# Threshold attention and a quick-GELU feed-forward in float32: scores transposed, values stationary for two heads, row maximum over partitions, tanh for sigmoid, 512-token blocks

## Chip, cores, metric

One core of one Trainium2 chip. The metric is the device time of one execution in microseconds (us), as the median of a kernel's fast runs.

## The reference

```python
q, k, v: (8, 8, 576, 64) float32;  tau = 0.02
scores = q @ k.T / 8
thresh = max(scores, -1) - tau
scores = where(scores >= thresh, scores, -1e9)
attn   = softmax(scores, -1)                    # the sum has 1e-9 added
x      = (attn @ v) as (4608 tokens, 512)
h      = x @ w_in                               # 512 x 2048
out    = (h * sigmoid(1.702 * h)) @ w_out       # 2048 x 512
```

The weights arrive as float64 words and are rounded to float32 on the chip. All matmuls run in float32.

## The kernel before

Queries lie on the partitions of the scores. A step handles 128 queries of two heads: scores, row maximum over the free dimension, exp, threshold with the row sum as accumulator, ten transposes of the weights on TensorE, then the values with the transposed weights stationary. Feed-forward units of batch b are woven between the steps of batch b+1.

```python
def row_max(sc):                                   # scores: queries x keys, in PSUM
    for h in range(2):
        nc.vector.tensor_reduce(out=nmax[:, h:h+1], in_=sc[h][:, :, 0:SH],
                                axis=AXL.XY, op=ALU.max, negate=True)
    ...
def exps(sc, bias):     # ScalarE: exp(scl * score + bias), from PSUM
def threshold(sc, thr, w):
    nc.vector.scalar_tensor_tensor(out=w[h], in0=sc[h][:, :, 0:SH], scalar=thr[:, h:h+1],
        in1=w[h], op0=ALU.is_ge, op1=ALU.mult, accum_out=den[:, h:h+1])
def transpose_w(w):     # 2 heads x (4 + 1) TensorE transposes of 128 x 128, then copies
def values(n, t, wT, rcp):
    for h in range(2):
        for c in range(NT):
            nc.tensor.matmul(pv[:, h, :], lhsT=wT[:, h, c, :], rhs=vr[:, h, ts(c, D)], ...)
    nc.vector.tensor_tensor(out=x, in0=pv, in1=rcp.to_broadcast([P, 2, D]), op=ALU.mult)
def gelu():                                        # after mm1 of one 128 x 384 hidden tile
    nc.scalar.activation(out=sig, in_=hps, func=AF.Sigmoid, scale=GELU_SCALE)
    nc.vector.tensor_tensor(out=gT[j], in0=hps, in1=sig, op=ALU.mult)
```

## Time and profile before

| | kernel before |
|---|---|
| median | 1957.6 us |
| TensorE busy | 96% |
| start, until the first feed-forward matmul | 258 us |
| middle, attention and feed-forward together | 1522 us |
| end, feed-forward alone | 175 us |

In the middle TensorE is busy 99.6% of the time, so TensorE's work sets the time there. The lines are in the prediction. PE is TensorE, DVE VectorE, ACT ScalarE, POOL GpSimd; PEclk is the share of the clock that TensorE was granted, in tenths; "idle before" on a line is how long the engine stood still just ahead of such instructions, and the arrow names what ended the wait.

### The profile page before, as it was taken

How to read it: one execution, taken by the hardware profiler on the slowest of the kernel's cores; microseconds unless marked ns; L12 is line 12 of the kernel's file. 1: busy time of each engine (PE TensorE's matmuls, PEld its weight loads, DVE VectorE, ACT ScalarE, POOL GpSimd, SP SyncE). 2: the span in 40 equal slices, each digit the busy share in tenths (PEclk: the TensorE clock that was granted, in tenths of full speed). 3: DMA queues.
4: the chain of work that ended last, by engine and by line, in shares of the span. 5: the costliest groups of instructions: out<-in, count | busy, mean ns of one | idle time of the engine just before them, and what ended most of it. 6: DMA issues, size and time to landing. Idle time of an engine off the chain costs nothing.

```text
span 1955.3 us, 23581 instructions
## 1 busy us (share of the span) xinstructions
PE 1870.5 (96%) x9248; PEld 1252.2 (64%) x9248; DVE 985.8 (50%) x2216; ACT 712.1 (36%) x1066; POOL 149.3 (8%) x422
## 2 busy tenths in 40 slices
PE   6776799999999999999999999999999999999999
PEld 4565677666666667666656667766656667766554
DVE  6888765555344355555435345555434445553110
ACT  2222255335325245334425336434424325432010
POOL 2333200000000000000000000000000000000000
PEclk8556599999999999999999999999999999999999
DMA  4323210101010000001010010000001010000000
GB/s 123 100 76 94 61 31 15 29 19 30 12 30 13 18 24 19 24 24 28 16 29 19 12 30 19 24 24 24 19 11 26 22 30 19 1 11 6 11 6 17
DMA packets 100160, 56.06 MB, mean 29 GB/s; under 512 B 83152, under 2 KB 91344, under 8 KB 100048
## 3 DMA queue, kind: packets, MB, share of 16 engines
q1 hardware_dynamic: 100048, 54.55, 10.0%
q8 instruction: 73, 1.20, 0.3%
q14 instruction: 39, 0.32, 0.1%
HBM read 45.09 MB, written 9.44 MB: 28 GB/s over the span
## 4 chain that ended last, share of the span: by engine, by line
PE 88%; DVE 9%; ACT 1%; issue 1%; POOL 1%; DMA 0%; SPq 0%; DVEq 0%; POOLq 0%; ACTq 0%
PE hps L310 25%; PE ops L329 25%; PE pv L278 16%; PE sc L204 9%; PE w_ps L261 7%; DVE frac L147 3%; PE x_ps L296 2%; PE w_ps L270 2%; DVE w L244 1%; DVE ex L173 1%; DVE qT L188 1%; DVE nmax L216 1%; PE qk_ps L187 1%; DVE ex L161 1%; DVE frac L143 1%
## 5 line engine op out<-in xcount | busy, mean ns | idle before, releaser
L310 PE MATMUL hps<-xT,w_in 128*128 128x384 f32 x1536 | 524.1, 487 | 0.0
L329 PE MATMUL ops<-w_out,gT 128*128 128x512 f32 x1152 | 515.7, 593 | 0.0
L278 PEld LDWEIGHTS pv<-v_raw,wT 128*128 128x128 f32 x3200 | 410.4, 206 | 46.8 <-DVE wT L262 14.2
L278 PE MATMUL pv<-v_raw,wT 128*128 128x64 f32 x3200 | 411.5, 287 | 10.9 <-DVE wT L262 10.1
L310 PEld LDWEIGHTS hps<-xT,w_in 128*128 128x128 f32 x1536 | 279.4, 190 | 161.4 <-issue 0.5
L329 PEld LDWEIGHTS ops<-w_out,gT 128*128 128x128 f32 x1152 | 209.5, 190 | 217.9 <-issue 217.1
L216 DVE TENSOR_REDUCE nmax<-sc 128x1 f32<-128x576 f32 x320 | 227.5, 752 | 145.0 <-PE sc L204 143.9
L234 ACT ACTIVATE w<-sc,bias,scl 128x576 f32<-128x576 f32 x320 | 248.5, 827 | 30.1 <-POOL bias L222 19.6
L244 DVE SCALAR_TENSOR_TENSOR w<-sc,thr,w 128x576 f32<-128x576 f32 x320 | 247.5, 811 | 6.9 <-ACT w L234 6.7
L204 PE MATMUL sc<-kT,qT 64*128 64x288 f32 x1280 | 219.9, 459 | 4.1 <-DVE w L244 3.8
L271 DVE COPY wT<-w_ps 128x256 f32<-128x256 f32 x160 | 67.6, 423 | 298.3 <-PE w_ps L270 298.3
L298 ACT COPY xT<-x_ps 128x128 f32<-128x128 f32 x128 | 50.5, 395 | 440.0 <-PE x_ps L296 440.0
L318 DVE TENSOR_TENSOR gT<-hps,sig 128x384 f32<-128x384 f32 x192 | 106.9, 557 | 177.0 <-ACT sig L317 170.8
L317 ACT ACTIVATE sig<-hps 128x384 f32<-128x384 f32 x192 | 94.1, 490 | 252.4 <-PE hps L310 250.4
L261 PE MATMUL w_ps<-ident,w 128*128 128x128 f32 x1280 | 177.9, 285 | 0.0
L204 PEld LDWEIGHTS sc<-kT,qT 64*128 64x128 f32 x1280 | 124.8, 201 | 57.7 <-issue 35.0
L261 PEld LDWEIGHTS w_ps<-ident,w 128*128 128x128 f32 x1280 | 156.5, 149 | 0.8 <-issue 0.8
L222 POOL TENSOR_SCALAR bias<-nmax,scl 128x2 f32<-128x2 f32 x160 | 41.7, 261 | 1338.7 <-DVE nmax L216 1297.0
L262 ACT COPY wT<-w_ps 128x512 f32<-128x512 f32 x160 | 94.1, 588 | 88.3 <-PE w_ps L261 88.3
L283 DVE TENSOR_TENSOR x<-pv,rcp 128x128 f32<-128x128 f32 x160 | 45.5, 284 | 143.7 <-PE pv L278 143.7
L270 PEld LDWEIGHTS w_ps<-ident,w 128*128 128x128 f32 x320 | 44.5, 145 | 104.2 <-issue 48.7
L262 DVE COPY wT<-w_ps 128x512 f32<-128x512 f32 x160 | 108.9, 681 | 1.1 <-PE w_ps L261 1.1
(44 smaller groups left out, 834.4 us busy)
## 6 DMA issues: line engine op xcount, KB each, us to landing
out_dram<-osb SPq DMA_DIRECT2D x36, 256.0 KB, 2.0
q_raw<-in_q_dram SPq DMA_DIRECT2D x64, 128.0 KB, 2.8
k_raw<-in_k_dram SPq DMA_DIRECT2D x64, 128.0 KB, 2.7
v_raw<-in_v_dram SPq DMA_DIRECT2D x32, 256.0 KB, 2.9
w<-in_moe_w_in_dram SPq DMA_DIRECT2D x16, 512.0 KB, 3.8
w<-in_moe_w_out_dram SPq DMA_DIRECT2D x16, 512.0 KB, 3.4
q_raw<-in_q_dram SPq DMA_DIRECT2D x32, 32.0 KB, 2.5
k_raw<-in_k_dram SPq DMA_DIRECT2D x32, 32.0 KB, 2.5
```

Of the source, the lines that this page charges most:

```text
L204: nc.tensor.matmul(sc[h][:, c, 0:SH], lhsT=qT[rows, ds(T0[t], P)], rhs=kT[rows, ts(c, SH)], start=True, stop=True,)
L216: nc.vector.tensor_reduce(out=nmax[:, h : h + 1], in_=sc[h][:, :, 0:SH], axis=AXL.XY, op=ALU.max, negate=True,)
L234: nc.scalar.activation(out=e, in_=sc[h][:, :, 0:SH], func=AF.Exp, bias=bias[:, h : h + 1], scale=scl,)
L244: nc.vector.scalar_tensor_tensor(out=w[h], in0=sc[h][:, :, 0:SH], scalar=thr[:, h : h + 1], in1=w[h], op0=ALU.is_ge, op1=ALU.mult, accum_o ...
L261: nc.tensor.transpose(p[:, c, :], flat(w, h)[:, ds(T0[c], P)], ident)
L262: (nc.vector.tensor_copy if h == 0 else nc.scalar.copy)(out=wT[:, h, 0:4, :], in_=p)
L270: nc.tensor.transpose(p[:, h, :], flat(w, h)[:, ds(T0[4], P)], ident)
L278: nc.tensor.matmul(pv[:, h, :], lhsT=wT[:, h, c, :], rhs=vr[:, h, ts(c, D)], start=(c == 0), stop=(c == NT - 1),)
L310: nc.tensor.matmul(hps, lhsT=w_in[:, c, ts(j, P)], rhs=xT[:, c, ds(c0, BLK)], start=(c == 0), stop=(c == NDC - 1),)
L317: nc.scalar.activation(out=sig, in_=hps, func=AF.Sigmoid, scale=GELU_SCALE)
L318: nc.vector.tensor_tensor(out=gT[j], in0=hps, in1=sig, op=ALU.mult)
L329: nc.tensor.matmul(ops, lhsT=gT[j][:, ts(i, P)], rhs=w_out[:, j, :], start=(j == 0), stop=(j == NFC - 1),)
```

## The change

The intent is to take work from TensorE. With keys on the partitions of the scores, the weights are already in the layout that the values' matmul needs, so no weight is transposed; and with 64 columns of v stationary, two heads share the array as two column tiles. The price is on the other engines: the maximum of a query now lies across partitions, the scores are copied to SBUF by ScalarE, the maximum is subtracted by DVE, and the row sums are added up by GpSimd over the key tiles. Tanh shares a table with exp: the changed kernel's trace has one table load, the one before 138.

```diff
+    def part_max(n, t):       # block-transposing maximum over 32 partitions
+        nc.vector.tensor_reduce(out=o, in_=i, axis=AXL.X, op=ALU.max, apply_transpose=True)
+    def max_a(n) ... max_c(n) # rest of the maximum: two small TensorE transposes, then
+        nc.vector.transpose(out=mb, in_=p2 broadcast)            # 128 x 1152
+    def sub(n, t):
+        nc.vector.tensor_tensor(out=s, in0=s, in1=mb, op=ALU.subtract)
+    def exps(n, t):           # ScalarE, SBUF to SBUF
+    def threshold(n, t):
+        nc.vector.scalar_tensor_tensor(out=s, in0=s, scalar=ntau, in1=e, op0=is_ge, op1=mult)
+    def values(n, t):
+        nc.tensor.matmul(pvs[n][ts(h, D), c, 0:SH], lhsT=v[:, t, h, :], rhs=w[:, h, ts(c, SH)], ...)
+    def add_w(n, t):
+        if t == 1:
+            nc.gpsimd.tensor_tensor(out=sums[n], in0=w[0], in1=w[1], op=ALU.add)
+        elif t < NKT:
+            nc.gpsimd.tensor_tensor(out=sums[n], in0=sums[n], in1=w[t], op=ALU.add)
+        else: ...             # the 64-row tail, one add for each head
+    def den_a(n):             # sums over partitions: ones stationary, 64 columns for each head
+    def place_x(n):
+        nc.vector.reciprocal(out=rc, in_=rc)                     # 128 x 576
+        nc.vector.tensor_tensor(out=xT[...], in0=pv[...], in1=rc[...], op=ALU.mult)
-    transposes of q, k, weights and x on TensorE, row_max over the free dimension
-            nc.scalar.activation(out=sig, in_=hps, func=AF.Sigmoid, scale=GELU_SCALE)
+            nc.scalar.activation(out=th, in_=hidden[0], func=AF.Tanh, scale=GELU_SCALE / 2)
+            nc.vector.scalar_tensor_tensor(out=gT[j], in0=th, scalar=1.0, in1=hidden[0], add, mult)
-    BLK = 384
+    BLK = 512
+    # one round handles pair m = n + 1 up to its weights, and the values of pair n;
+    # each call has a place from 0 to 18 and the calls are issued in order of place:
+            at(1.5 * t, scores, m, t); at(1.5 * t + 1.0, part_max, m, t)
+        at(8.0, max_a, m); at(8.2, max_b, m); at(9.0, max_c, m)
+            at(9.3 + 1.2 * t, sub, m, t); at(9.6 + 1.2 * t, exps, m, t)
+            at(11.0 + 1.2 * t, threshold, m, t)
+        at(12.0, prep, m + 1, 0); at(12.6, prep, m + 1, 1)
+            at(1.5 * t + 0.7, values, n, t); at(0.1 * t, add_w, n, t)
+        at(8.5, den_a, n); at(9.6, place_x, n)
+            at(LEN * (u + 0.5) / due, *units[u])                 # feed-forward, evenly
```

(Loads, weight conversion and bookkeeping left out.)

## The prediction

> **What bounds the kernel now.** I read the page's busy shares and slices first, then busy time by stretch, then TensorE's timeline over one step, then the groups by shape.
>
> ```profile
> PE 1870.5 (96%) x9248; PEld 1252.2 (64%) x9248; DVE 985.8 (50%) x2216; ACT 712.1 (36%) x1066; POOL 149.3 (8%) x422
> ...
> PE   6776799999999999999999999999999999999999
> ...
> PEclk8556599999999999999999999999999999999999
> ```
>
> After the sixth slice TensorE is never free and has its full clock. The first hps matmul starts at 258 us, so I cut the span there and where attention ends. The columns are length, busy time of PE, PEld, DVE, ACT, POOL, then clock and DMA:
>
> ```profile
> 0.00:258.00 258.00, 183.56 (x849) 148.22 (x850) 203.97 (x403) 72.51 (x125) 74.03 (x119) 0.66 0.31 89
> 258.00:1780.00 1522.00, 1515.87 (x7923) 1015.07 (x7922) 758.50 (x1773) 621.97 (x908) 75.29 (x303) 1.00 0.08 21
> 1780.00:1955.00 175.00, 171.10 (x479) 88.88 (x477) 23.36 (x42) 17.62 (x35) 0.00 (x0) 1.00 0.03 11
> ```
>
> So 258 us of start (batch 0's attention and the weight conversion, DVE busy 79%, clock 0.66), 1522 us in which TensorE is the bound (attention of batch b+1 with the feed-forward of batch b), and 175 us of feed-forward alone. Busy PE overlaps itself, so costs are read as start-to-start spacings:
>
> ```profile
> 999.49 0.89 PE L204 MATMUL sc<-kT,qT 64*128 64x288 f32 x6
> 1000.32 0.33 PE L296 MATMUL x_ps<-ident,x 128*128 128x128 f32 x1
> 1000.48 1.04 PE L261 MATMUL w_ps<-ident,w 128*128 128x128 f32 x8
> 1001.36 3.60 PE L329 MATMUL ops<-w_out,gT 128*128 128x512 f32 x8
> 1004.79 0.38 PE L270 MATMUL w_ps<-ident,w 128*128 128x128 f32 x2
> 1005.01 3.60 PE L329 MATMUL ops<-w_out,gT 128*128 128x512 f32 x8
> 1008.45 2.34 PE L278 MATMUL pv<-v_raw,wT 128*128 128x64 f32 x20
> 1010.62 3.65 PE L329 MATMUL ops<-w_out,gT 128*128 128x512 f32 x8
> ```
>
> A float32 matmul leaves two records. Eight records of 512 columns take 3.43 to 3.45 us, 0.43 us each, or 0.84 ns per column. Twenty pv records take 2.17 us, 0.11 us each though they stream only 64 columns: their 128x128 weight load sets the pace. Eight transposes take 0.88 us, 0.11 each. A full step's eight sc records take 1.17 us; each 288-column record alone would need 0.24 us, so two heads on different rows of the array run side by side (four pairs at 0.245 = 0.98) and 0.19 us goes at the change to the next group. Prep's transposes, per pair, are ten of 0.11 plus waits.
>
> **What the Trainium skill says.**
> 1. "TensorEngine Tiling (Array Packing)", § Performance Considerations and § Key Properties: with at most 64 stationary columns the array splits into column tiles that run in parallel (up to 2x), and changing the tiling mode drains TensorE. For row tiles the trace agrees (0.98 us for four pairs, 0.1 to 0.2 us at each change). Column tiles do not occur in the kernel before, in float32 or otherwise.
> 2. "SBUF — State Buffer", § Who interferes with whom: a DVE instruction with two SBUF inputs and a GpSimd one that reads SBUF lock each other out for a whole instruction; a reduce does not. The trace agrees: the same instruction takes 0.69 us alone and 1.63 us when it starts behind a GpSimd one that lasts until 27.86 us.
>
> ```profile
> 23.48 0.69 DVE L147 SCALAR_TENSOR_TENSOR frac<-w,frac 128x512 uint32<-128x512 uint32 x1
> ...
> 26.78 1.63 DVE L147 SCALAR_TENSOR_TENSOR frac<-w,frac 128x512 uint32<-128x512 uint32 x1
> ...
> 26.56 1.30 POOL L177 TENSOR_TENSOR w_in<-mant,ex 128x512 f32<-128x512 f32 x1 [0.88 <-DVE ex L173]
> ```
>
> 3. "ScalarE: Activation LUTs", § Table sets: exp and tanh share a set, sigmoid's set lacks exp. The trace shows 138 loads of 1.283 us in alternation (L317 69, L234 68, one at the start). The built changed kernel has one.
> 4. "VectorE: DVE Perf Modes", § First, the fixed hardware budget: Reciprocal iterates with a repeat count of 8. The trace has it only on two elements (0.17 us), so it says nothing.
>
> **The change on TensorE, per pair of heads** (32 pairs). Removed: 40 weight transposes 40 x 0.11 + 10 tail ones = 5.4 us; 100 pv records 2.26 us per step with its edges = 11.3; x transposes 5 x 0.165 = 0.8; prep about 1.5. With scores 5 x 1.17 = 5.8 the old attention costs 24.8 us, which agrees with the stretch: 1692 us after 258, less feed-forward 1536 x 0.326 + 1152 x 0.432 = 998, over 28 pairs.
>
> Added: scores stay about as many: 32 records in 16 pairs 3.9, block-diagonal tail 4 x 0.245 = 1.0. Values: 40 records of 288 columns; side by side 20 x 0.245 = 4.9, one after another 9.8. Row sums over partitions by ones: 8 records, 1.0. Two small transposes 0.6. About ten changes of tiling at 0.3 for entry and exit: 3.0. Sum 14.4 us, saving 10.4 per pair. Feed-forward has the same columns; 384 wide costs 0.326 x 1536 = 501, 512 wide 1152 x 0.43 = 495: 6 us saved.
>
> **The change on the others, per pair.** DVE at 1.04 ns per element plus 0.07 us (the 512-element two-input instruction above: 0.61 us to its successor): block transposes of q and k 1.35; partial maxima over partitions 4 x 1.27 + 0.67 = 5.8; the maximum's chain, with an 1152-wide broadcast transpose, 2.1; subtraction 4 x 1.27 + 2 x 0.67 = 6.4; threshold 5.8; placing 0.9; reciprocal of 576 elements 0.7, or 4.9 if eight cycles each. That is 23 to 27 us, and 2.5 for gelu. ScalarE: score copies 9 x 0.6, exps 5.3, row sums 0.65, tanh and output 3: 15. GpSimd: 1.30/512 = 2.55 ns per element: three adds of 2.9 and two of 1.5, 12 us. In the middle stretch a pair has 110 us x 7 blocks / 28 = 27.5 us of feed-forward beside 14.4 of attention, 42 us: TensorE stays the bound on average.
>
> It is not spread evenly. The changed order puts all scores and values in the first half of an iteration, and max chain, subtraction, exp, threshold in the second, where TensorE has only eight units of feed-forward (13.7 us) and DVE 16.5 to 21 us. In iterations that do the second matmul nothing waits for DVE. In those that do the first (14 of 28), four gelus stand between DVE's long instructions: between two of them lie thr, sub, prep, thr, prep, sub, some 7 us, against 3.44 us of one hidden tile, with two PSUM tiles. That makes a stall of 3 (fast reciprocal) to 7 us in each: 14 x 5 = 70 us.
>
> **Start.** Five rounds before the first feed-forward. Round one: loads (16 small transfers, packets of 128 bytes) and a bare chain, about 40 us. Then four rounds of DVE-bound work: 23 to 27 attention, 8 conversions of 256 columns x 1.1 = 9, locked out by GpSimd's 12 us of adds and the conversions 6 to 8, waits for the slow-clock TensorE 4: 45 us. Together 220 us, against 258. Conversions go on in the first three pairs with feed-forward, 10 each: about 12 us of delay.
>
> **Sum.** Start 220; delay 12; middle 7 x 110 + 27.5 x 14.4 = 1166; stalls 70; last two blocks 223. Total 1691, about 1695. The old kernel ended with two blocks of 384 (175 us), the new with two of 512, but TensorE's total is what counts.
>
> **Rivals.**
> - *Column tiles don't run side by side in float32.* Values and sums lose 5.9 us per pair: 1695 + 27.5 x 5.9 = 1860. For: no such matmul in the trace. Against: the row-tiled float32 pairs do run side by side. 1 in 6.
> - *DVE becomes the bound in the middle.* If block transposes or the transposing maximum run at half rate, DVE gains 8 us a pair: 36 to 40 against 42, stalls double or triple, and the start grows by 40: about 1830. The trace has no such instruction. 1 in 8.
> - *TensorE hides everything.* If the reciprocal is fast and PSUM buffers absorb the bunching, stalls vanish: 1600 to 1620. For: the old middle stretch is 99.6% busy in spite of DVE in each step. 1 in 4.
> - *Table loads as the gain* (177 us of ScalarE): no, it is 36% busy and TensorE never waits for it in the middle.
>
> **Range and chances.** 1600 to 1810 spans the third rival and most of the second. To miss 2% faster (1918) both the first and second must come together with more. Faster 0.95, same 0.03, slower 0.02.
>
> **What would show it.** Pairs of pv records starting together at 0.245 us (or one by one); the reciprocal's mean (0.7 or 4.9 us); block transposes and transposing maxima near 0.7 and 1.3 us; first hps near 220 us; PE waits before hps on gT in half of the iterations; two blocks alone at the end in 223 us; GpSimd adds near 3 us. A start over 280 us, or attention over 20 us of TensorE per pair, would make the prediction wrong.

## The result and the profile after

The changed kernel takes 1937.4 us (1935.1 to 1942.0) and is correct. Ratios here are the mean time of one kernel's fast runs over that of the other's fast runs of the same rounds, so not quite the ratio of the medians: 0.991, interval 0.989 to 0.993. The prediction was 1695 us, with a range up to 1810.

The page of the changed kernel:

```profile
PE 1596.7 (83%) x5056; PEld 688.1 (36%) x5056; DVE 1271.3 (66%) x1300; ACT 500.4 (26%) x725; POOL 553.2 (29%) x427
...
PE   4344477779888998899889998898889988999999
...
PEclk9766688889999998899999988999999988999999
```

TensorE's records fell from 9248 to 5056 and its busy share from 96% to 83%. It has holes throughout, and its clock, which was at full speed from the seventh slice on, now dips again and again. Busy time by stretch, cut at the first hps matmul and after the last pair's row sums (length, then PE, PEld, DVE, ACT, POOL, clock, DMA):

```profile
0.00:247.00 247.00, 107.36 (x391) 54.07 (x392) 222.86 (x274) 71.72 (x108) 125.28 (x144) 0.71 0.24 59
247.00:1697.00 1450.00, 1255.17 (x4120) 530.75 (x4121) 1021.77 (x991) 403.51 (x575) 427.94 (x283) 0.93 0.12 26
1697.00:1935.00 238.00, 234.13 (x548) 103.28 (x544) 26.62 (x36) 25.13 (x42) 0.00 (x0) 1.00 0.03 11
```

The predicted sum had 220, 1248 (1166 of TensorE, 70 of stalls, 12 of conversions) and 223 us. So 202 of the 242 missing microseconds are in the middle. There TensorE stands idle for 195 us, and its busy time too is above the estimate. The groups of the changed kernel:

```profile
L305 DVE SCALAR_TENSOR_TENSOR s_m<-s_m,ntau,e 128x1152 f32<-128x1152 f32 x128 | 237.6, 1856 | 1.0
L361 DVE RECIPROCAL rc<-rc 128x576 f32<-128x576 f32 x32 | 119.8, 3745 | 12.5 <-ACT rc L352 12.5
L291 DVE TENSOR_TENSOR s_t<-s_t,mb 64x576 f32<-64x576 f32 x64 | 107.1, 1673 | 0.4
L305 DVE SCALAR_TENSOR_TENSOR s_t<-s_t,ntau,e 128x576 f32<-128x576 f32 x32 | 52.6, 1643 | 0.0
L382 PE MATMUL hps<-xT,w_in 128*128 128x512 f32 x1152 | 583.8, 652 | 95.1 <-DVE gT L390 95.1
```

A 576-element subtraction on 64 partitions takes longer than a 1152-element one on 128 (1.67 against 1.35 us): that is no work, that is waiting inside the instruction. The timelines of DVE and of GpSimd over the same end of one round show for what:

```profile
1003.09 3.77 DVE L305 SCALAR_TENSOR_TENSOR s_m<-s_m,ntau,e 128x1152 f32<-128x1152 f32 x1
1006.78 3.83 DVE L291 TENSOR_TENSOR s_t<-s_t,mb 64x576 f32<-64x576 f32 x2
1010.65 1.42 DVE L305 SCALAR_TENSOR_TENSOR s_m<-s_m,ntau,e 128x1152 f32<-128x1152 f32 x1
...
1012.61 2.84 DVE L305 SCALAR_TENSOR_TENSOR s_t<-s_t,ntau,e 128x576 f32<-128x576 f32 x1
```

```profile
1003.02 2.62 POOL L331 TENSOR_TENSOR ws<-s_m 128x1152 f32<-128x1152 f32 x1
1007.03 2.97 POOL L333 TENSOR_TENSOR ws<-ws,s_m 128x1152 f32<-128x1152 f32 x1 [1.39 <-DVE s_m L305]
1012.21 2.62 POOL L333 TENSOR_TENSOR ws<-ws,s_m 128x1152 f32<-128x1152 f32 x1 [2.21 <-DVE s_m L305]
```

The threshold that starts 0.07 us behind the first add takes 3.77 us; one with no add beside it takes 1.42. The adds have places at the head of the *next* round, but a place only orders each engine's own queue. The two weight tiles that the first add needs were done by 1000.65, and all that stood before it in GpSimd's queue was a copy of k's tail (1001.40 to 1002.95). So it started at 1003.02, in the middle of DVE's busiest stretch. TensorE, in the same stretch:

```profile
996.11 5.36 PE L382 MATMUL hps<-xT,w_in 128*128 128x512 f32 x8 [2.32 <-DVE gT L390]
1003.23 3.70 PE L382 MATMUL hps<-xT,w_in 128*128 128x512 f32 x8 [1.76 <-DVE gT L390]
1006.86 1.24 PE L224 MATMUL ps<-qkT 64*128 64x288 f32 x8
1012.75 3.44 PE L398 MATMUL ops<-w_out,gT 128*128 128x512 f32 x4 [4.65 <-DVE gT L390]
```

It waits for gelus (gT), and the four records after the longest wait take 3.44 us, 0.85 us from one to the next, twice the 0.43 of the others: the clock is halved. The Trainium skill, "TensorE: Matmul & The Clock Gate", § HAM oscillation, warns of this for idle gaps of more than some 3.4 us. The trace agrees for the gap of 4.65 us, but the one of 2.32 us above is followed by half clock as well (eight records in 5.36 us, against 3.70 behind the gap of 1.76), so the page's figure is not the limit here. 0.93 is the granted clock of the middle.

Rounds without gelus wait as well. ScalarE's timeline in one:

```profile
1061.55 0.77 ACT L300 ACTIVATE e<-s_t,scl 128x576 f32<-128x576 f32 x1 [3.88 <-DVE s_t L291]
...
1062.71 1.17 ACT L230 COPY s_m<-ps 128x576 f32<-128x576 f32 x2
```

ScalarE's queue holds the tail's exp, which waits 3.88 us for DVE's locked subtraction, and behind it the copies of the next round's scores. TensorE's next scores then waited 3.88 us for them (ended at 1063.39).

### The profile page after: what moved, and what is told of

Its sections match the earlier page's. It is cut to its first block, busy times and chain, and to the rows that moved or that the text cites. A ratio compares the mean times of both kernels' runs of the same rounds, so it can differ in the third digit from the quotient of the medians.

```text
span 1934.9 us, 14193 instructions
## 1 busy us (share of the span) xinstructions
PE 1596.7 (83%) x5056; PEld 688.1 (36%) x5056; DVE 1271.3 (66%) x1300; ACT 500.4 (26%) x725; POOL 553.2 (29%) x427
## 4 chain that ended last, share of the span: by engine, by line
PE 50%; DVE 44%; issue 2%; ACT 2%; POOL 0%; SPq 0%; DVEq 0%; DMA 0%; ACTq 0%; POOLq 0%
PE ops L398 18%; PE hps L382 16%; DVE s_m L305 9%; DVE s_m L288 8%; PE pv L321 7%; PE ps L224 6%; DVE rc L361 6%; DVE s_t L291 5%; DVE frac L151 3%; DVE ex L177 2%; DVE qkT L195 2%; DVE mb L279 2%; DVE gT L390 2%; PE ps L213 2%; DVE frac L147 2%
## 5 line engine op out<-in xcount | busy, mean ns | idle before, releaser
L382 PE MATMUL hps<-xT,w_in 128*128 128x512 f32 x1152 | 583.8, 652 | 95.1 <-DVE gT L390 95.1
L224 PE MATMUL ps<-qkT 64*128 64x288 f32 x1024 | 211.1, 496 | 196.6 <-ACT s_m L230 105.2
L245 DVE TRANSPOSE_TENSOR_REDUCE pmax<-s_m 128x36 f32<-128x1152 f32 x128 | 172.8, 1364 | 117.6 <-ACT s_m L230 117.6
L300 ACT ACTIVATE e<-s_m,scl 128x1152 f32<-128x1152 f32 x128 | 160.7, 1256 | 331.4 <-DVE s_m L288 331.4
L305 DVE SCALAR_TENSOR_TENSOR s_m<-s_m,ntau,e 128x1152 f32<-128x1152 f32 x128 | 237.6, 1856 | 1.0
L230 ACT COPY s_m<-ps 128x576 f32<-128x576 f32 x256 | 151.8, 640 | 260.7 <-PE ps L224 260.7
L333 POOL TENSOR_TENSOR ws<-ws,s_m 128x1152 f32<-128x1152 f32 x64 | 183.6, 2868 | 64.6 <-DVE s_m L305 63.1
L288 DVE TENSOR_TENSOR s_m<-s_m,mb 128x1152 f32<-128x1152 f32 x128 | 172.4, 1348 | 2.5
L321 PE MATMUL pv<-s_m,v_m 128*64 128x288 f32 x1024 | 173.4, 465 | 0.0
L361 DVE RECIPROCAL rc<-rc 128x576 f32<-128x576 f32 x32 | 119.8, 3745 | 12.5 <-ACT rc L352 12.5
```

The lines of the kernel that those rows point to most:

```text
L224: nc.tensor.matmul(ps[h][:, c, 0:SH], lhsT=kT[ts(h, D), ts(t, P)], rhs=qT[ts(h, D), ts(c, SH)], start=True, stop=True,)
L230: nc.scalar.copy(out=halves(st[:, h, :]), in_=ps[h][:, :, 0:SH])
L245: nc.vector.tensor_reduce(out=o, in_=i, axis=AXL.X, op=ALU.max, apply_transpose=True)
L288: nc.vector.tensor_tensor(out=s, in0=s, in1=mb, op=ALU.subtract)
L300: nc.scalar.activation(out=e, in_=s, func=AF.Exp, scale=scl)
L305: nc.vector.scalar_tensor_tensor(out=s, in0=s, scalar=ntau, in1=es.pop((n, t)), op0=ALU.is_ge, op1=ALU.mult)
```

## The experiments

Each was timed three times over beside the kernel before, which measured 1953 to 1958 us throughout; a few microseconds between two runs are not read. Below, a round of the kernel is the distance between the row sums of successive pairs. It opens with DVE's crowded half (subtraction to threshold) and is called after the feed-forward matmuls, first or second, that TensorE has there. "Middle" and "idle" are cut as above.

| run | us | ratio to before | middle | TensorE idle in it |
|---|---|---|---|---|
| changed kernel | 1937.4 | 0.991 | 1451 | 195 |
| e1_adds_late | 1811.7 | 0.927 | 1334 | 114 |
| e2_place_early | 1974.5 | 1.008 | 1478 | 229 |
| e3_skew | 1918.7 | 0.980 | 1413 | 197 |
| e4_no_adds (wrong) | 1755.5 | 0.897 | 1301 | 100 |
| e5_sigmoid | 1965.8 | 1.004 | 1480 | 217 |
| e6_blk384 | 1982.5 | 1.014 | 1553 | 241 |
| e7_late_skew | 1814.5 | 0.927 | 1308 | 127 |
| e8_late_spread | 1908.8 | 0.975 | 1417 | 167 |
| e9_all_late | 1862.4 | 0.952 | 1375 | 136 |
| e10_defer | 1790.5 | 0.916 | 1298 | 91 |
| e11_late_no_recip (wrong) | 1716.9 | 0.878 | 1242 | 63 |
| e13_late_defer | 1763.3 | 0.903 | 1275 | 80 |
| e14_late_first | 1768.1 | 0.905 | 1295 | 105 |
| e15_late_defer_first | 1723.9 | 0.882 | 1251 | 73 |

**e1_adds_late.** The sums start from the fourth weight tile instead of the first, so the first add has to wait for it.

```diff
-            nc.gpsimd.tensor_tensor(out=sums[n], in0=w[0], in1=w[1], op=ALU.add)
+            nc.gpsimd.tensor_tensor(out=sums[n], in0=w[3], in1=w[0], op=ALU.add)
...
-            nc.gpsimd.tensor_tensor(out=sums[n], in0=sums[n], in1=w[t], op=ALU.add)
+            nc.gpsimd.tensor_tensor(out=sums[n], in0=sums[n], in1=w[t - 1], op=ALU.add)
```

> GpSimd's first add of a pair now needs the fourth weight tile instead of the first two, so it can start only when nearly all thresholds are done. Lock theory (GpSimd's adds and DVE's two-input instructions shut each other out, and DVE's late half-iteration holds TensorE): the mean of DVE's 1152-wide thresholds falls from 1.86 to about 1.42 us and of the 64-partition subtractions from 1.67 to about 0.8, DVE loses about 150 us of busy time, and the kernel takes 1740 to 1800 us. Rival (DVE's own work, bunched in the half of the iteration where TensorE has only eight units, is what holds it): the means fall just the same, but the time stays above 1880 us.

1811.7 us, 126 us less, with the same instructions. The groups:

```profile
L305 DVE SCALAR_TENSOR_TENSOR s_m<-s_m,ntau,e 128x1152 f32<-128x1152 f32 x128 | 179.9, 1405 | 1.0
...
L291 DVE TENSOR_TENSOR s_t<-s_t,mb 64x576 f32<-64x576 f32 x64 | 49.0, 766 | 0.4
```

The waiting inside DVE's instructions is gone from these two. The gain fell 12 us short of the expected span (up to 1800): the tail's threshold still meets the first add (1.58 us against 0.81 alone), and other stalls remain.

**e4_no_adds.** The sums are the first weight tile, and GpSimd adds nothing. Its output is wrong, which doesn't matter for the time.

```diff
     def add_w(n, t):
-        ...
+        sums[n] = sT[n][0]
```

> Wrong result on purpose: the row sums are taken from the first weight tile alone, so GpSimd adds nothing at all. It is the upper limit of what the lock costs. Lock theory: 1730 to 1790 us, and within 20 us of the late adds if lateness takes the whole lock away. Rival: above 1880 us.

1755.5 us, so the adds cost 182 us of the changed kernel. Lateness takes away 126 of it; it was not within 20 us as expected. About 32 us of the rest lie in the start, which falls from 247 to 216 us: there the adds meet the weight conversion. The tail's threshold, without an add beside it:

```profile
L305 DVE SCALAR_TENSOR_TENSOR s_t<-s_t,ntau,e 128x576 f32<-128x576 f32 x32 | 25.9, 811 | 0.0
```

Rounds with second matmuls fall from 48 or more to 44.1 us, those with first matmuls from 54 or 55 to 47.9.

**e2_place_early.** Row sums and placing ahead of the maximum's chain.

```diff
-            at(8.5, den_a, n)
-            at(9.6, place_x, n)
+            at(6.75, den_a, n)
+            at(7.1, place_x, n)
```

> Row sums, reciprocal and placing move ahead of the maximum's chain, into the half of the iteration where DVE has gaps; no work is removed. Bunching theory: 4.7 us a pair leave the crowded half, so 100 to 150 us are saved, 1790 to 1840 us. Lock theory alone: the crowded half is set by the waits on GpSimd, which stay, so less than 60 us are saved, above 1880 us.

1974.5 us: above 1880, as the lock theory had it, but slower than the changed kernel, which neither foresaw. The waits of TensorE say why:

```profile
PE p L257 <- DVE mx L255: 151.0, 32, 6.5
```

In every round TensorE stood up to 6.5 us at the maximum's transpose, because the reciprocal had moved directly ahead of it in DVE's queue. So the run does not tell the two theories apart; it only shows that DVE's first half has gaps, but not there.

**e3_skew and e7_late_skew.** More feed-forward units in the second half of the round, without and with late adds.

```diff
-                at(LEN * (u + 0.5) / due, *units[u])
+                at(LEN * ((u + 0.5) / due) ** 0.6, *units[u])
```

> The same feed-forward units, but 11 of 16 instead of 8 in the half of the iteration in which DVE is crowded. Bunching theory: TensorE has 19 instead of 14 us of work there and idles 3 to 5 us less per pair, 1800 to 1860 us. If DVE's in-order queue holds every gelu up whatever the place, nothing is gained or it is lost again in the first-matmul iterations: 1920 to 1960 us.

> The late adds with 11 of 16 feed-forward units in the crowded half. If after the lock the rest of the stalls is DVE's own work bunched, this gains where the skew alone gained 18 us: 1740 to 1790 us against 1812. If gelus in DVE's queue are the limit whatever the places, it stays at 1800 to 1820.

1918.7 and 1814.5 us. The first gains 19 us, less than expected for bunching and more than for none; the second gains nothing over e1. In the later blocks, rounds with second matmuls become shorter (44.2 us in e1, 41.4 and 43.7 in e7) and rounds with first matmuls longer (48.0 to 50.9 and 48.6), since more gelus then stand in DVE's crowded half. Where DVE must take part in the shifted work, shifting it did not help.

**e8_late_spread.** Late adds, and the attention's places moved so that subtraction to threshold take 10 places of 18 instead of 6.5.

```diff
-                at(1.5 * t, scores, m, t)                 # part_max, max_a..c, exps moved likewise
-                at(9.3 + 1.2 * t, sub, m, t)
-                at(11.0 + 1.2 * t, threshold, m, t)
+                at(1.0 * t, scores, m, t)
+                at(6.7 + 2.0 * t, sub, m, t)
+                at(8.6 + 2.0 * t, threshold, m, t)
```

> The late adds, and the attention's places moved instead of the feed-forward's: scores and partial maxima in the first 5 of 18 places, the maximum's chain at 5.4 to 6.4, subtractions to thresholds spread over 6.7 to 16.6 in place of 9.3 to 15.8. No instruction added or removed. Bunching theory: DVE's work lies more evenly beside TensorE's and most of the 114 us of idle TensorE in the middle goes: 1690 to 1760 us. Rival (the latency of the chain, not the bunching): 1800 us or more.

1908.8 us, a miss of the experiment's own making, visible in one group:

```profile
L291 DVE TENSOR_TENSOR s_t<-s_t,mb 64x576 f32<-64x576 f32 x64 | 108.3, 1692 | 0.4
```

The new places put the tail's subtraction behind the fourth threshold, which releases the first add, so the lock was back. It says nothing on bunching.

**e5_sigmoid.** One part undone.

```diff
-            nc.scalar.activation(out=th, in_=hidden[0], func=AF.Tanh, scale=GELU_SCALE / 2)
+            nc.scalar.activation(out=th, in_=hidden[0], func=AF.Sigmoid, scale=GELU_SCALE)
```

(and a plain multiply, and no factor 0.5 at the output)

> One part of the change undone: sigmoid and a plain multiply again, the rest as changed, so exp and sigmoid alternate on ScalarE with a table load at each turn (a hundred or more loads of 1.28 us). If ScalarE's in-order queue is part of the chain that holds TensorE (its exps stand between DVE's subtraction and threshold), the time rises by 20 to 60 us over the changed kernel, to 1955 to 2000 us. If ScalarE has room enough, it stays within 10 us of 1937.

1965.8 us, 28 us slower, with 100 table loads of 1.283 us. Tanh does pay here, though ScalarE is busy only 26%: the loads lie in the queue between DVE's subtraction and its threshold.

**e6_blk384.** The other part undone: blocks of 384, one more buffer for the attention result.

```diff
-    BLK = 512
+    BLK = 384
```

> One part of the change undone: blocks of 384 tokens again (and one more buffer for the attention result, which such blocks need). TensorE then has ten blocks of 83 us, not seven of 110, beside the attention, and two of 83 instead of two of 110 after it. If the middle is set by DVE's crowded half and the locks, some 60 us of feed-forward move from the end into time in which TensorE idles: 1880 to 1930 us. If it is set by TensorE's sum, nothing changes but 6 us for the narrower matmuls: 1935 to 1950 us.

1982.5 us, 45 us slower, against both expectations. More feed-forward does lie in the middle, but with narrow tiles TensorE waits more for gelus:

```profile
L382 PE MATMUL hps<-xT,w_in 128*128 128x384 f32 x1536 | 616.3, 546 | 160.6 <-DVE gT L390 160.6
```

160.6 us against 95.1: a tile of 384 covers 2.6 us of TensorE work, one of 512 covers 3.4. That DVE's queue takes as long in either is the likely reason; it was not tested apart.

**e11_late_no_recip.** e1 without the reciprocal. Its output is wrong, which doesn't matter for the time.

```diff
-        nc.vector.reciprocal(out=rc, in_=rc)
```

> Wrong result on purpose: the late adds without the reciprocal (results are multiplied by the sums). Size of the reciprocal's 3.75 us of DVE per pair, 120 us in all. Bunching theory: 60 to 110 us less than the late adds, 1700 to 1750 us. If DVE has slack: within 20 us of 1812.

1716.9 us: 95 us less than e1 for 120 us of DVE instructions. DVE's amount of work in the crowded half is thus the second cause, beside the lock.

**e9_all_late.** e1, with the tail tile handled ahead of the fourth weight tile, so that the add comes behind every threshold.

```diff
-            for t in range(NKT + 1):
-                at(9.3 + 1.2 * t, sub, m, t)                 # exps, threshold likewise
+            for i, t in enumerate([0, 1, 2, 4, 3]):
+                at(9.3 + 1.2 * i, sub, m, t)
```

> As the late adds, but the 64-row tail tile is subtracted, exponentiated and thresholded ahead of the fourth weight tile, so that GpSimd's first add comes behind every threshold. Lock theory: the tail's threshold falls from 1.58 to 0.81 us too, and 10 to 25 us more are saved than by the late adds: 1785 to 1805 us. What remains above the 1755 us of the run without adds is the lock against the weight conversion in the first seven rounds (31 us of start).

1862.4 us, 51 us slower than e1, although the tail's threshold fell to 0.83 us as expected. From the end of the maximum's chain (start of mb) to the copies of the next scores, one second-matmul round of this run has 19.8 us and one of e1 19.3, and the first add starts 21.1 us behind mb in place of 19.6. TensorE's idle time in the middle rises by 22 us, its busy time for the same matmuls by 19 (granted clock 0.94 against 0.96). Which of these small delays starts it is not settled; how they grow is in the clock record. Past the first 430 us TensorE's wait in a second-matmul round is 2.1 to 2.4 us here and 1.55 to 1.85 in e1, and half clock follows 11 of the 12 such waits here, but 4 of 12 in e1.

**e10_defer and e13_late_defer.** In three of four rounds ScalarE copies the values' sum to its place, and reciprocal and scaling follow in the next round's first half, where DVE has gaps; e10 with the order of e9, e13 with that of e1. To make room, the sums get a buffer of their own and the conversion's frac has one buffer in place of two (not shown below).

```diff
+            if n % NPAIR != NPAIR - 1:             # in den_a
+                for x, pv, _ in pieces_of_x(n):
+                    nc.scalar.copy(out=x, in_=pv)
-            at(9.6, place_x, n)
+            if n % NPAIR == NPAIR - 1:
+                at(9.6, place_x, n)
+            if n % NPAIR != 0:
+                at(4.9, recip, n - 1)
+                at(6.4, place_x, n - 1)            # scales in place
```

> All late, and in three of four rounds the reciprocal and the scaling of a pair move out of the crowded half into the next round's first half: ScalarE copies the values' sum to the attention result at once, and DVE scales it there. The same instructions plus three small copies on ScalarE. Bunching theory: 4.8 us a pair leave the crowded half in 24 of 32 rounds, and unlike the run with early placing no wait of TensorE for the maximum stands behind them: 60 to 110 us are saved, 1690 to 1740 us. If it lands before TensorE's wait for the maximum again, above 1780 us.

> The late adds and the deferred reciprocal together, with the tail tile in its old order again. If the all-late order lost because its last exp is the wide one and the next round's score copies stand behind it on ScalarE, this is faster than the deferred kernel with that order (1790 us): 1735 to 1760 us. If the order made no difference, 1785 to 1795 us.

1790.5 and 1763.3 us. Against their bases (e9, e1) they save 72 and 48 us with no arithmetic removed: moving DVE's work out of the crowded half is enough. Both miss their spans on the slow side, e13 by 3 us. e10 lands above 1780, where its rival put it: TensorE's waits for the maximum do rise, from 12 to 32 us (to 31 in e13), nearly all of it before the weight conversion ends. The order alone accounts for 27 us between them, so it does matter, with the reservation above.

**e14_late_first and e15_late_defer_first.** The block transposes and the next pair's first scores are issued earlier, so that their copies stand ahead of the last two exps in ScalarE's queue; without and with the deferral.

```diff
-            at(12.0, prep, m + 1, 0)
-            at(12.6, prep, m + 1, 1)
+            at(6.5, prep, m + 1, 0)
+            at(8.3, prep, m + 1, 1)
+            at(13.0, scores, m + 1, 0)             # t = 0 dropped from the next round
```

> The late adds, with the next pair's block transposes and first scores moved ahead (places 6.5, 8.3 and 13.0 of 18), so that ScalarE copies these scores before the last two exps, and TensorE need not wait for them. ScalarE-queue theory: TensorE's waits for score copies (40 us in the middle of the late-adds run) mostly go, and 1.5 us of DVE leaves the crowded half: 1740 to 1785 us. Rival: only DVE's amount of work in the crowded half counts, and the waits turn up before the next scores or the gelus: 1795 to 1815 us.

> All three: late adds, deferred reciprocal, early transposes and first scores. If the three causes (lock, DVE's crowded half, ScalarE's queue) are separate, the gains add: 1690 to 1730 us, near what TensorE's own work allows (start 247, 28 rounds of 42 us, end 233: 1656 us). If the later two are the same wait seen twice, it is no better than the deferred one: 1735 to 1760 us.

1768.1 us, 44 less than e1, and 1723.9 us, 39 less than e13. So the deferral's 48 us and this change's 44 all but add (88 of 92). Past the first 422 us TensorE's waits for score copies, 19 us in e1, are gone in e14 and in e15. The early issue also takes 1.5 us of DVE work from the crowded half, so the queue's own share of the gain is not separated. e15 is correct, and it is the fastest correct kernel here, 12% faster than the kernel before. Its page and its middle stretch:

```profile
PE   5544467776999999999999999999999999999999
...
PEclk9565668988999999999999999999999999999999
```

```profile
235.00:1486.00 1251.00, 1177.71 (x4123) 504.08 (x4124) 925.70 (x1006) 421.03 (x644) 386.98 (x288) 0.98 0.14 31
```

Past the tenth slice TensorE is full and at full clock, and rounds take 41.7 to 44.1 us. It does the middle's matmuls in 1178 us of busy time; the changed kernel needed 1255 us for the same ones. By the clock records TensorE was busy at half clock for 184 us of the changed kernel's middle and for 44 us of this one's. Half of that is lost, 92 and 22 us: the clock explains 70 of the 77 us between them. Most of what is still lost here lies before the tenth slice, where weights are converted: 54 of the middle's 73 us of idle TensorE, and all of its half clock.

## Why the prediction was wrong

*What held.* The change on TensorE was sized well. Column tiles do run side by side in float32: eight pv records go by in 1.12 us, 0.14 us each, where one 288-column record alone needs 0.24. The rival that doubted it fell.

```profile
1020.51 1.19 PE L321 MATMUL pv<-s_m,v_m 128*64 128x288 f32 x8
1021.63 0.70 PE L398 MATMUL ops<-w_out,gT 128*128 128x512 f32 x1
```

The predicted 42 us of TensorE per pair are the 41.7 us of the best rounds of e15, and 1166 us for the middle are 1178. The 512-wide feed-forward matmul has its 0.43 us. The block transposes and transposing maxima run at full rate (0.77 and 1.36 us), so the second rival's condition fell too, though DVE did come to set the time of half a round, by another way. The third rival, that TensorE hides everything, fell with 195 us of idle TensorE; whether more buffers for the hidden tile would have absorbed waits was not tried. The reciprocal is the slow kind, 3.75 us (4.9 was the upper estimate). Neither of the prediction's own signs of being wrong came up: the start stayed under 280 us and attention under 20 us of TensorE per pair.

*What failed* is the term of the stalls, "14 x 5 = 70 us", with the 12 us of delay beside it. In place of these 82 us the middle lost 272: 195 us of idle TensorE, and 77 us more of busy time than e15 needs for the same matmuls. Five things under it were wrong.

1. The lock was foreseen and put into the start only. For the middle the prediction charged GpSimd's 12 us of adds to no one. They have places at the head of the next round, where DVE does maxima, which an add leaves alone (two took 2.62 us beside one at 1065.81). They ran with DVE's two-input instructions instead, for the queues run ahead of the places. Measured as count times (mean less the mean without adds): 128 x 0.45 + 64 x 0.91 + 32 x 0.83 = 142 us of waiting inside DVE's instructions. Removing the adds saves 182 us, making them late 126.
2. "In iterations that do the second matmul nothing waits for DVE." They took 48 us and more, not 42. TensorE waited there for score copies that stand in ScalarE's queue behind an exp that waits for DVE. Without the adds they take 44.1 us, and with early scores 41.7 and 42.4.
3. In the first-matmul rounds the stall was foreseen as 3 to 7 us, from 16.5 to 21 us of DVE work. DVE was busy for all but 0.2 us of that stretch's 28.7 (986.8 to 1015.5 us of the trace). The slow reciprocal is in the 21 already. The lock adds 6.7 us (3.77, 3.83 and 2.84 us above, against 1.41, 1.53 and 0.81 by the means without adds), the gelus 2.2. The round takes 54 us, 12 more than 42. Without the adds it is 47.9 us, a stall of 6: that part was right.
4. The slowing of TensorE after such waits was not counted at all: 92 us lost at half clock in the middle, 70 more than in e15. A kernel whose TensorE was all but never idle became one where it is idle for 2 to 5 us at a time.
5. The 12 us of delay by the weight conversion were too few. From the first hps matmul to the seventh pair's row sums (247 to 421 us) 401 TensorE records take 174 us; at e15's later pace (3719 records in 1062 us) they would take about 115, an estimate. Some 60 us are lost there, where delay and stalls had about 22, and some 70 in e15 (189 us for 405 records). One conversion takes DVE 2.81 us (0.64 + 0.97 + 0.34 + 0.86 in the mean), 1.88 without the adds; the prediction had 1.1, and 6 to 8 us of lock in a round of the start.

In sum the middle was 1450 us: 1178 of matmuls as e15 does them, 195 of idle TensorE, 77 of slower matmuls. The start's 247 us against 220 are the conversion again: its later rounds take 52 to 53 us, not 45, and eight conversions at 2.81 us are 22.5 us where the prediction had 9 and at most 8 of lock. Without the adds a round there takes 44.5 us and the start 216, so the 220 fit a start without the lock that was counted in them. The end's 238 against 223 is mostly the rest of the last round, which the cut at the last row sums leaves in it.

So most of the expected gain was there on TensorE, and was given back in DVE's queue: first by locks with GpSimd, then by DVE's own work bunched in half a round, then again by the clock. That "TensorE stays the bound on average" was true and of no use; each round has a half in which it is not.

## What to carry to other kernels

When work moves off the bound engine, add up the receiving engines' work by stretch of the round, not over the round, and hold it against what the bound engine has to do in that stretch. A place in program order does not keep an instruction of an idle engine from running early; if it must not meet another engine's work, give it a data dependence that makes it wait, as the order of one addition did here (126 us). A few microseconds of TensorE idling cost more than themselves, since the clock can fall behind them: 92 us at the changed kernel's 195 of idling in the middle.

## What the Trainium skill lacked or had wrong

- "VectorE: DVE Perf Modes", § First, the fixed hardware budget, gives a repeat count of 8 for Reciprocal but no time: 576 float32 elements took 3.745 us, 6.5 ns each, where a threshold over 1152 took 1.405.
- The same page has no time for a maximum with a transpose in it: 1152 elements took 1.36 us, as much as a plain two-input instruction.
- "TensorEngine Tiling (Array Packing)", § Key Properties, says that a change of tiling mode drains TensorE, not what it costs: some 0.1 us on entry and 0.2 on the way back to the full array. It does not say whether column tiles run in parallel in float32; they do (1.12 us for eight records).
- "SBUF — State Buffer", § Who interferes with whom, is right on the lock (3.77 us against 1.42).
- "TensorE: Matmul & The Clock Gate", § HAM oscillation, puts the harm at idle gaps of more than some 3.4 us; shorter ones were enough here. In the changed kernel, from 421 us to the end of the middle, half clock followed all 36 waits of TensorE of 2.3 us or more and none of the 12 of 1.7 to 1.9 us; in e1 it followed some of 1.55.
